# Kernel feature attention and SoLU layer on one core: query maxima joined by a DMA round trip, variance by ScalarE squares

## The chip, the cores and the metric

One core of one Trainium2 chip runs one program. The core has TensorE (PE in the profile, its weight loads PEld), VectorE (DVE), ScalarE (ACT), GpSimd (POOL), SyncE (SP, which here only issues DMAs) and 16 DMA engines. The metric is the device time of one execution in microseconds; lower is better.

## The reference

```python
def phi(x):                                   # x: [8, 8, 576, 64]
    proj = np.einsum('bhsd,df->bhsf', x, w_phi)              # 128 features
    proj = proj - np.max(np.abs(proj), axis=-1, keepdims=True)
    return np.concatenate([np.exp(proj), np.exp(-proj)], axis=-1)
q_p, k_p = phi(q), phi(k)
kv = np.einsum('bhsf,bhsd->bhfd', k_p, v);  z = np.sum(k_p, axis=2)
num = np.einsum('bhsf,bhfd->bhsd', q_p, kv)
den = np.einsum('bhsf,bhf->bhs', q_p, z)[..., None] + 1e-06
x = (num / den)                               # -> 4608 tokens x 512
h = x @ w_in                                  # 512 -> 1024
e = np.exp(h - h.max(-1));  sm = e / (e.sum(-1) + 1e-09);  solu = h * sm
var = np.mean((solu - mu) ** 2, axis=-1)      # mu: mean of solu over 1024
out = ((solu - mu) / np.sqrt(var + 1e-06) * g_ln) @ w_out    # 1024 -> 512
```

## The kernel before

The work has two halves that run interleaved. The attention half goes over 16 units u (a batch and one of two groups of four heads), and each unit has two halves `sub` of two heads each. The second half, called moe in the code, goes over 36 tiles t of 128 tokens. Each step is an `op` with a name, an engine, a cost that a planner had used, and the names of the ops that it follows. The tuple `SEQUENCE` is a list of op numbers: it is the order in which the ops are written into the program, and with it the order of every engine's queue. The same walk gives out the buffers of each tag (`SBUF_BUFS`, `PSUM_BUFS`), so a buffer is reused in that order too. All matrix products in the split parts are made of three `fp32r` products of high and low parts.

Names in the profile: `pjk` is a projection of keys and `pq` one of queries (units 3 to 15, transposed, 128 features on the partitions and 288 tokens along the row). `visit` is one TensorE group per half: `num` and `den` of the half before, `kvT` of this one. `h` is the first product of a moe tile (24 matmuls in two halves), `o` the second one (24 matmuls). `uT` is TensorE's transposition of the last tiles (t from 33); the other tiles are transposed by `ub` (VectorE, 32x32 blocks) and a DMA round trip `du`, `uTs`, and then split into `uhs` and `uls`. The PSUM tag `a` has three banks; `pjk`, `pq`, `num`, `den`, `mtp` and `mcp` share them. The tag `h` has one buffer of two banks, and it is free again when `moe_u` has read it.

The maximum over features for a query half (26 of them, units 3 to 15). VectorE transposes `pq` in 32x32 blocks to `blk`, where a partition p = 32 q + t holds the 32 features of quadrant q of a token t. `q_max4` takes the maximum of absolute values inside each quadrant, `m4` of 128x36. The four quadrants of each token must then meet: `q_mt` transposes `m4` on TensorE (`mtp`), `q_max` takes the maximum over the four (`mt`), `q_mb` copies it four times on GpSimd (`mb`), `q_mc` transposes back on TensorE (`mcp`), and `q_mcol` copies it on ScalarE (`mcol`). `q_sub` subtracts it on GpSimd, VectorE transposes back (`pT`), and ScalarE takes the exponentials `fq` that the next visit reads.

The variance in a moe tile. `moe_u` forms h times e on VectorE (`eu`). `moe_var` takes `bn_stats` of its two halves and `bn_aggr` on VectorE (`bst`, `mv`). `moe_scale` makes, on GpSimd, (variance + (1e-3 (sum + 1e-9))^2) to the power -1/2 in four small instructions (`sa`, `sa`, `sa`, `sc`). Only `moe_oe`, the scaled copy of `o` out of PSUM on ScalarE (`os`), waits for `sc`. The mean itself need not be subtracted there, since `w_out` is centred beforehand.

Of the kernel before, what the change touches and what calls it, by code (L numbers as in the profile page):

```python
# [8 lines left out]
F32 = mybir.dt.float32  # L9
# [11 lines left out]
P = 128  # L21
# [19 lines left out]
    rk=4, rv=5, xh=2, xl=2, m=3, d=3, e=6, za=2, kf=2, q4=5, m4=2, mt=2, mb=2, E=2, dE=2, rb=2,  # L41
    xa=1, xb=1, m2k=5, big=8, nm=2, sm=3, bst=2, mv=2, sa=2, sc=3,
# [242 lines left out]
def linear_attention_then_moe(ctx: ExitStack, tc, qT, qT2, kT, v, w_phi, w_in, g_ln, w_out, out):  # L285
# [54 lines left out]
    nc.gpsimd.memset(ones_half, 0.0)  # L340
    for i in range(2):
        nc.gpsimd.memset(ones_half[i * D : (i + 1) * D, i], 1.0)

    mb_tiles = []
    for i in range(SBUF_BUFS["mb"]):
        mb_tiles.append(const.tile([P, 4, 32], F32, name=f"mb{i}"))
# [921 lines left out]
```

## Time and profile before

| what | value |
|---|---|
| time, median of 3 runs (lowest, highest) | 742.18 us (741.92, 743.12) |
| the profiled execution | 742.26 us, span 740.4 us |
| PE busy | 716.5 us, 97% of the span, 4671 matmuls |
| DVE / ACT / POOL busy | 545.4 / 377.1 / 485.2 us |
| DMA | 109.96 MB, 149 GB/s, 51.7% of 16 engines |

Matmuls overlap in the records: one that is shown with 400 ns starts 0.23 us after its neighbour. The distance between starts, or the chain of waits, tells what a matmul costs the queue; the mean ns of one does not. All lines read L273, since one helper issues every instruction; groups are told apart by the names of tiles.

### The profile page before, as it was taken

Reading aid. Unit: us, or ns where it says so; the run is one execution under the profiler, and the core shown is the slowest. Engines: PE = TensorE matmul, PEld = TensorE weight load, DVE = VectorE, ACT = ScalarE, POOL = GpSimd, SP = SyncE. Lnnn points to the kernel's source line nnn. Section 1 sums busy time; section 2 is a strip of 40 time slices with the busy share of each in tenths; the row PEclk is TensorE's granted clock in tenths of the full one; section 3 lists DMA queues with packets and bytes.
Section 4 is the critical chain, followed back from the end, with each engine's and each line's share of the span. In section 5 each row is a group of like instructions: output and inputs, shape, how many; then the busy total and the mean of one; then the engine's idle time right before and its main releaser. Section 6 shows DMA issues by size and latency. Waiting matters only on the chain. (4 is left out here: it accounts for less than half of the span.)

```text
span 740.4 us, 13275 instructions
## 1 busy us (share of the span) xinstructions
PE 716.5 (97%) x4671; PEld 533.0 (72%) x4671; DVE 545.4 (74%) x861; ACT 377.1 (51%) x717; POOL 485.2 (66%) x507
## 2 busy tenths in 40 slices
PE   6999989999999999999999999999999999999997
PEld 4666767677667777777777777776777677778886
DVE  6999879776768787869769687669777876627651
ACT  3795665544644563645456545535644552424231
POOL 1126799985888878777778885977757867033210
PEclk9999999999999999999999999999999999999999
DMA  7874446652845675555566555563744353511241
GB/s 225 283 239 100 133 131 167 174 156 68 212 112 146 187 212 153 159 136 162 151 172 181 149 153 156 153 191 96 209 130 133 101 161 95 158 40 57 86 150 64
DMA packets 123730, 109.96 MB, mean 149 GB/s; under 512 B 58768, under 2 KB 109968, under 8 KB 123152
## 3 DMA queue, kind: packets, MB, share of 16 engines
q1 hardware_dynamic: 123664, 109.11, 51.7%
q8 instruction: 37, 0.61, 0.4%
q14 instruction: 29, 0.24, 0.1%
HBM read 76.68 MB, written 32.39 MB: 147 GB/s over the span
## 5 line engine op out<-in xcount | busy, mean ns | idle before, releaser
L273 POOL TENSOR_TENSOR zacc<-zacc,ek 128x512 f32<-128x512 f32 (+1 forms) x78 | 107.6, 1379 | 27.4 <-ACT ek L273 23.2
L273 ACT ACTIVATE ek<-dk 128x512 f32<-128x512 f32 (+1 forms) x160 | 90.0, 585 | 51.0 <-DVE dk L273 47.8
L273 PE MATMUL o<-w_out_h,uls 128*128 128x512 f32 x264 | 104.9, 397 | 2.3 <-DVE uls L273 2.3
L273 PE MATMUL o<-w_out_h,uhs 128*128 128x512 f32 x264 | 105.3, 399 | 0.0
L273 PE MATMUL o<-w_out_l,uhs 128*128 128x512 f32 x264 | 104.3, 395 | 0.0
L273 PE MATMUL h<-win_h,mxh 128*128 128x512 f32 x288 | 92.2, 401 | 0.2 <-DVE eu L273 0.2
L273 PE MATMUL h<-win_h,mxl 128*128 128x512 f32 x288 | 90.8, 396 | 0.0
L273 PE MATMUL h<-win_l,mxh 128*128 128x512 f32 x288 | 90.7, 396 | 0.0
L273 ACT ACTIVATE fq<-pT 128x576 f32<-128x576 f32 x104 | 68.5, 679 | 40.2 <-DVE pT L273 39.8
L273 POOL TENSOR_TENSOR hq<-rawq,hq 64x1152 fp32r<-64x1152 f32 x26 | 70.3, 2704 | 6.2 <-ACT hq L273 3.4
L273 ACT ACTIVATE eu<-h,nm 128x1024 f32<-128x1024 f32 x36 | 40.1, 1113 | 66.1 <-DVE nm L273 58.7
L273 DVE TENSOR_TENSOR uls<-uTs,uhs 128x1024 fp32r<-128x1024 f32 x33 | 56.6, 1714 | 20.5 <-ACT uhs L273 19.5
L273 DVE TENSOR_REDUCE m<-pjk 128x4 f32<-128x512 f32 (+1 forms) x80 | 49.4, 620 | 28.2 <-PE pjk L273 27.7
L273 PE MATMUL num<-fq,kvf 128*64 128x288 f32 x512 | 69.2, 412 | 0.4 <-DMA kvf<-dk 0.2
L273 POOL TENSOR_TENSOR xa<-E,rb 128x576 f32<-128x576 f32 (+1 forms) x32 | 30.4, 953 | 58.0 <-DMA rb<-d 36.4
L273 PEld LDWEIGHTS h<-win_h,mxl 128*128 128x128 f32 x288 | 54.4, 189 | 13.1
L273 PE MATMUL kvT<-ek,rawv 128*64 128x256 f32 x512 | 63.8, 380 | 0.0
L273 DVE TENSOR_REDUCE nm<-h 128x1 f32<-128x1024 f32 x36 | 43.6, 1212 | 27.0 <-PE h L273 26.9
L273 PEld LDWEIGHTS h<-win_l,mxh 128*128 128x128 f32 x288 | 54.2, 188 | 13.0
L273 PEld LDWEIGHTS o<-w_out_h,uls 128*128 128x128 f32 x264 | 49.6, 188 | 16.6 <-DVE uls L273 4.9
L273 DVE TENSOR_TENSOR eu<-h,eu 128x1024 f32<-128x1024 f32 x36 | 43.7, 1214 | 23.4 <-ACT eu L273 23.1
L273 POOL TENSOR_TENSOR xl<-rawk,xh 128x256 fp32r<-128x256 f32 (+1 forms) x65 | 46.2, 714 | 21.6 <-ACT xh L273 20.9
(116 smaller groups left out, 1593.4 us busy)
## 6 DMA issues: line engine op xcount, KB each, us to landing
du<-ub SPq DMA_DIRECT2D x33, 512.0 KB, 2.9
uTs<-du SPq DMA_DIRECT2D x132, 128.0 KB, 3.2
rawq<-in_q SPq DMA_DIRECT2D x26, 576.0 KB, 4.7
rb<-d SPq DMA_DIRECT2D x64, 144.0 KB, 3.7
out<-os SPq DMA_DIRECT2D x36, 256.0 KB, 2.7
rawk<-in_k SPq DMA_DIRECT2D x64, 128.0 KB, 2.9
rawv<-in_v SPq DMA_DIRECT2D x64, 128.0 KB, 3.1
dk<-kvs SPq DMA_DIRECT2D x28, 192.0 KB, 2.2
```

Source lines behind the costliest of these rows:

```text
L273: return self.tc.keep_in_program_order(method(*args, **kwargs))
```

## The change

The 26 query maxima meet by a DMA round trip: `q_mout` writes `m4` to a scratch `dm` in DRAM in the order token, quadrant, column; `q_min` reads for each token all four quadrants (144 numbers) into each of the four partitions that need them (`mq4`); `q_max` takes the maximum over the four on VectorE and gives `mcol` at once. Both DMAs are in SP's queue. The two transpositions, the GpSimd copy and the ScalarE copy go. In the moe half `moe_u` becomes a `scalar_tensor_tensor` that also sums its product (`su`); `moe_var` runs on ScalarE: a small product `nb` that makes minus the mean (scaled by 2^-5), and a `Square` of 1024 elements in place over `eu` with its sum `mv`; it follows the transposition that reads `eu`. `moe_denom`, two small instructions on VectorE (`sa`), takes the place of three GpSimd ones; the power stays on GpSimd. Some tags get more buffers (`m4`, `sm`, `bst`, `mv`, `sa`, `sc`, a new `nb`), `mb` goes. `SEQUENCE` is written anew, with 2811 numbers in place of 2827; only its first line is shown, since the numbers tell a reader nothing.

```diff
-    rk=4, rv=5, xh=2, xl=2, m=3, d=3, e=6, za=2, kf=2, q4=5, m4=2, mt=2, mb=2, E=2, dE=2, rb=2,
-    xa=1, xb=1, m2k=5, big=8, nm=2, sm=3, bst=2, mv=2, sa=2, sc=3,
+    rk=4, rv=5, xh=2, xl=2, m=3, d=3, e=6, za=2, kf=2, q4=5, m4=4, mt=2, E=2, dE=2, rb=2,
+    xa=1, xb=1, m2k=5, big=8, nm=2, sm=5, bst=4, nb=3, mv=4, sa=3, sc=4,
...
 SEQUENCE = (
-    3, 95, 0, 2, 136, 102, 132, 7, 97, 105, 140, 98, 133, 99, 88, 89, 106, 103, 107, 137, 117, 134, 135, 8, 144,
+    3, 95, 0, 2, 136, 132, 7, 102, 97, 103, 133, 140, 98, 111, 99, 195, 100, 137, 117, 134, 101, 96, 135, 8,
...
-    def q_mt(st, sub):
-        st["mtp", sub] = bank("a", [P, 512], "mtp")
-        nc.tensor.transpose(out=st["mtp", sub][:NM, :P], in_=st["m4", sub], identity=ident)
+    def q_mout(st, sub):
+        st["dm", sub] = dram.tile([32, 4, NM], F32, tag="dm", name="dm")
+        nc.sync.dma_start(out=st["dm", sub].rearrange("t q c -> q t c"), in_=st["m4", sub])
+
+    def q_min(st, sub):
+        st["mq4", sub] = sb("mt", [P, 4 * NM], name="mq4")
+        src = st["dm", sub].rearrange("t q c -> t (q c)").unsqueeze(0)
+        nc.sync.dma_start(out=st["mq4", sub], in_=src.to_broadcast([4, 32, 4 * NM]))
...
     def q_max(st, sub):
-        st["mt", sub] = sb("mt", [NM, 32])
+        st["mc", sub] = sb("m4", [P, NM], name="mcol")
         nc.vector.tensor_reduce(
-            out=st["mt", sub], in_=st["mtp", sub][:NM, :P].rearrange("c (q t) -> c t q", q=4), axis=AX.X,
-            op=ALU.max,
+            out=st["mc", sub], in_=st["mq4", sub].rearrange("p (q c) -> p c q", q=4), axis=AX.X, op=ALU.max
         )
-    def q_mb(st, sub):
-
-        mb = st["mb", sub] = mb_tiles[plan.slot[st["u"], "mb", sub]]
-        nc.gpsimd.tensor_copy(out=mb[:NM], in_=st["mt", sub].unsqueeze(1).to_broadcast([NM, 4, 32]))
-
-    def q_mc(st, sub):
-        st["mcp", sub] = bank("a", [P, 512], "mcp")
-        nc.tensor.transpose(
-            out=st["mcp", sub][:, :P], in_=st["mb", sub].rearrange("c q t -> c (q t)"), identity=ident
-        )
-
-    def q_mcol(st, sub):
-        st["mc", sub] = sb("m4", [P, NM], name="mcol")
-        nc.scalar.copy(out=st["mc", sub], in_=st["mcp", sub][:, :NM])
...
     def moe_u(t):
-        nc.vector.tensor_tensor(out=M["e", t], in0=M["h", t], in1=M["e", t], op=ALU.mult)
+        M["su", t] = sb("bst", [P, 1], name="su")
+        nc.vector.scalar_tensor_tensor(
+            out=M["e", t], in0=M["h", t], scalar=1.0, in1=M["e", t], op0=ALU.mult, op1=ALU.mult, accum_out=M["su", t]
+        )
     def moe_var(t):
-        st = sb("bst", [P, 2, 6])
-        for i in range(2):
-            nc.vector.bn_stats(out=st[:, i, :], in_=M["e", t][:, i * 512 : (i + 1) * 512])
-        M["mv", t] = sb("mv", [P, 2])
-        nc.vector.bn_aggr(out=M["mv", t], in_=st)
+        nb = sb("nb", [P, 1])
+        M["mv", t] = sb("mv", [P, 1])
+        nc.scalar.mul(out=nb, in_=M["su", t], mul=-(2.0**-15))
+        nc.scalar.activation(
+            out=M["e", t], in_=M["e", t], func=AF.Square, scale=2.0**-5, bias=nb, accum_out=M["mv", t]
+        )
+    def moe_denom(t):
+        a = M["sa", t] = sb("sa", [P, 1])
+        nc.vector.tensor_scalar(out=a, in0=M["sm", t], scalar1=1e-9, scalar2=1e-3, op0=ALU.add, op1=ALU.mult)
+        nc.vector.scalar_tensor_tensor(out=a, in0=a, scalar=a, in1=M["mv", t], op0=ALU.mult, op1=ALU.add)
     def moe_scale(t):
-        a = sb("sa", [P, 1])
         M["sc", t] = sb("sc", [P, 1])
-        nc.gpsimd.tensor_scalar(out=a, in0=M["sm", t], scalar1=1e-9, scalar2=1e-3, op0=ALU.add, op1=ALU.mult)
-        nc.gpsimd.tensor_tensor(out=a, in0=a, in1=a, op=ALU.mult)
-        nc.gpsimd.tensor_tensor(out=a, in0=a, in1=M["mv", t][:, 1:2], op=ALU.add)
-        nc.gpsimd.tensor_tensor(out=M["sc", t], in0=a, in1=neg_half, op=ALU.pow)
+        nc.gpsimd.tensor_tensor(out=M["sc", t], in0=M["sa", t], in1=neg_half, op=ALU.pow)
...
-        op(n("var"), "vector", 2 * dve(512) + 200, z + 12, moe_var, (t,), [n("u")],
-           [("bst", n("bst")), ("mv", n("mv"))], [n("e")])
-        op(n("sc"), "gpsimd", 1340, z + 14, moe_scale, (t,), [n("var")], [("sa", n("sa")), ("sc", n("sc"))],
-           [n("sm"), n("mv")])
+        op(n("var"), "scalar", act(DF) + 168, z + 12, moe_var, (t,),
+           [n("tb")] if t < TURN_PE else [n("t", 0), n("t", 1)], [("nb", n("nb")), ("mv", n("mv"))], [n("e"), n("su")])
+        op(n("sa"), "vector", 310, z + 14, moe_denom, (t,), [n("var")], [("sa", n("sa"))], [n("sm"), n("mv")])
+        op(n("sc"), "gpsimd", 520, z + 14.5, moe_scale, (t,), [n("sa")], [("sc", n("sc"))], [n("sa")])
```

How the change moves instructions is seen at three places. TensorE, before, in unit 14: the last matmul of a key projection, then the transposition of a query half's maxima (`mtp`), a tile's `h`, and two `pq` whose banks come after it.

```order
L273 MATMUL pjk<-wph_h,xl 128x256
L273 MATMUL mtp<-ident,m_6921 36x128
L273 MATMUL h<-win_h,mxh 128x512 x2
L273 MATMUL h<-win_l,mxh 128x512 x2
L273 MATMUL h<-win_h,mxl 128x512 x2
L273 MATMUL h<-win_h,mxh 128x512 x2
L273 MATMUL h<-win_l,mxh 128x512 x2
L273 MATMUL h<-win_h,mxl 128x512 x2
L273 MATMUL pq<-hq,w_hh 128x288
```

TensorE, after, at the like place of unit 14, behind the visit's `den`:

```order
L272 MATMUL den<-fq,kvf 32x288 x8
L272 MATMUL pq<-hq,w_hh 128x288
L272 MATMUL pq<-hq,w_l_88 128x288
L272 MATMUL pjk<-wph_h,xh 128x256
L272 MATMUL pjk<-wph_l,xh 128x256
L272 MATMUL pjk<-wph_h,xl 128x256
```

No transposition stands among the matmuls any more; the groups of `h`, `o`, `pjk`, `pq` and the visits are all there, in much the same rotation.

VectorE, before, from a query half's `q_max4` (`m_6855`) to the maximum over the quadrants (`mt`):

```order
L273 TENSOR_REDUCE m_6855<-blk 128x36
L273 TENSOR_TENSOR uls<-uTs,uhs 128x1024
L273 STREAM_TRANSPOSE blk<-pq 128x288
L273 TENSOR_REDUCE m<-pjk 128x4
L273 TENSOR_REDUCE mt<-mtp 36x32
```

VectorE, after, from `q_max4` of a half (`m_6751`) to its `mcol`, which now waits for a DMA:

```order
L272 TENSOR_REDUCE m_6751<-blk 128x36
L272 STREAM_TRANSPOSE blk<-pq 128x288 x3
L272 TENSOR_REDUCE m_6775<-blk 128x36
L272 TENSOR_REDUCE nm<-h 128x1
L272 TENSOR_TENSOR uls<-uTs,uhs 128x1024
L272 SCALAR_TENSOR_TENSOR eu,su<-h,eu 128x1024
L272 STREAM_TRANSPOSE ub<-eu 128x8x4x32
L272 TENSOR_REDUCE mcol<-mq_6841 128x36
```

More work of VectorE stands between the two maxima than before, and no `bst` or `mv` rows stand among it.

SP's queue, before, around the load of a query half in unit 14 or 15 (`d` and `rb` are the reciprocals of `den`, `vz` and `rawv` values):

```order
L273 DMA rawq<-in_q 128x1152
L273 DMA d_6787<-cmr 128x9
L273 DMA du<-ub 128x1024
L273 DMA rawv<-in_v 128x256
L273 DMA uTs<-du 32x4x256
```

SP's queue, after, with the two round trips of unit 14:

```order
L272 DMA dm<-m_6751 4x32x36
L272 DMA out<-os 128x512
L272 DMA uTs<-du 32x4x256
L272 DMA rb<-d_6621 64x2x288 x2
L272 DMA mq_6841<-dm 128x1x144
L272 DMA dm<-m_6775 4x32x36
L272 DMA uTs<-du 32x4x256
L272 DMA rawq<-in_q 128x1152
L272 DMA mq_6848<-dm 128x1x144
L272 DMA rawv<-in_v 128x256
```

The two DMAs of a round trip stand in the queue with other transfers between them, and whatever comes later waits behind them.

More of the change, by code (lines that the diff above doesn't have):

```diff
@@ L342, in linear_attention_then_moe @@
         nc.gpsimd.memset(ones_half[i * D : (i + 1) * D, i], 1.0)
-    mb_tiles = []
-    for i in range(SBUF_BUFS["mb"]):
-        mb_tiles.append(const.tile([P, 4, 32], F32, name=f"mb{i}"))
-        nc.gpsimd.memset(mb_tiles[i], 0.0)
     win_h = const.tile([P, DM // P, DF], F32R, name="win_h")
@@ L985, in linear_attention_then_moe @@
                 add(("qm4", sub), "vector", dve(2 * S), z, q_max4, (sub,), prev, [("m4", ("m4", sub))], [("blk", sub)])
-                add(("qmt", sub), "tensor", mm(128), z + 0.3, q_mt, (sub,), [("qm4", sub)], [("a", ("mtp", sub))],
-                    [("m4", sub)])
-                add(("qmx", sub), "vector", 200, z + 0.4, q_max, (sub,), [("qmt", sub)], [("mt", ("mt", sub))],
-                    [("mtp", sub)])
-                add(("qmb", sub), "gpsimd", 400, z + 0.5, q_mb, (sub,), [("qmx", sub)], [("mb", ("mb", sub))],
-                    [("mt", sub)])
-                add(("qmc", sub), "tensor", mm(128), z + 0.7, q_mc, (sub,), [("qmb", sub)], [("a", ("mcp", sub))],
-                    [("mb", sub)])
-                add(("qml", sub), "scalar", 90, z + 0.8, q_mcol, (sub,), [("qmc", sub)], [("m4", ("mc", sub))],
-                    [("mcp", sub)])
-                add(("qs", sub), "gpsimd", 2070, z + 1, q_sub, (sub,), [("qml", sub)], (), [("blk", sub), ("mc", sub)])
+                add(("qmo", sub), "sync", (380, 450), z + 0.3, q_mout, (sub,), [("qm4", sub)], (), [("m4", sub)])
+                add(("qmi", sub), "sync", (440, 1000), z + 0.5, q_min, (sub,), [("qmo", sub)], [("mt", ("mt", sub))])
+                add(("qmx", sub), "vector", 230, z + 0.8, q_max, (sub,), [("qmi", sub)], [("m4", ("mc", sub))],
+                    [("mt", sub)])
+                add(("qs", sub), "gpsimd", 2070, z + 1, q_sub, (sub,), [("qmx", sub)], (), [("blk", sub), ("mc", sub)])
             for c in range(2):
@@ L1193, in linear_attention_then_moe @@
            [(e_tag, n("e")), ("sm", n("sm"))], [n("h"), n("nm")])
-        op(n("u"), "vector", dve(DF), z + 7, moe_u, (t,), [n("ex")], (), [n("h"), n("e")])
-        op(n("var"), "vector", 2 * dve(512) + 200, z + 12, moe_var, (t,), [n("u")],
-           [("bst", n("bst")), ("mv", n("mv"))], [n("e")])
-        op(n("sc"), "gpsimd", 1340, z + 14, moe_scale, (t,), [n("var")], [("sa", n("sa")), ("sc", n("sc"))],
-           [n("sm"), n("mv")])
+        op(n("u"), "vector", dve(DF) + 65, z + 7, moe_u, (t,), [n("ex")], [("bst", n("su"))], [n("h"), n("e")])
+        op(n("var"), "scalar", act(DF) + 168, z + 12, moe_var, (t,),
+           [n("tb")] if t < TURN_PE else [n("t", 0), n("t", 1)], [("nb", n("nb")), ("mv", n("mv"))], [n("e"), n("su")])
+        op(n("sa"), "vector", 310, z + 14, moe_denom, (t,), [n("var")], [("sa", n("sa"))], [n("sm"), n("mv")])
+        op(n("sc"), "gpsimd", 520, z + 14.5, moe_scale, (t,), [n("sa")], [("sc", n("sc"))], [n("sa")])
         by_dma = t < TURN_PE
```

293 rows, old and new, of the table SEQUENCE are left out of this document.

## The prediction

> **What bounds the kernel.** I read the page first, for the shares, then the windows, for where TensorE idles, then TensorE's own waits, then the chain of waits, for what one instruction costs the queue, and last the groups.
>
> ```profile
> PE 716.5 (97%) x4671; PEld 533.0 (72%) x4671; DVE 545.4 (74%) x861; ACT 377.1 (51%) x717; POOL 485.2 (66%) x507
> PEclk9999999999999999999999999999999999999999
> ```
>
> TensorE is busy for 97% of the span at the full granted clock; the other engines have a quarter of their time or more free. The windows (PE, PEld, DVE, ACT, POOL busy, granted clock, DMA share, GB/s) say where the rest of TensorE's time is.
>
> ```profile
> 0.00:100.00 100.00, 89.41 (x782) 62.28 (x782) 86.47 (x129) 66.93 (x141) 42.55 (x41) 1.00 0.63 191
> 100.00:640.00 540.00, 531.08 (x3452) 394.84 (x3451) 412.35 (x675) 282.24 (x532) 419.59 (x419) 1.00 0.55 152
> 640.00:700.00 60.00, 59.43 (x281) 46.59 (x281) 30.56 (x35) 17.52 (x30) 18.93 (x34) 1.00 0.27 83
> 700.00:741.00 41.00, 36.62 (x162) 29.32 (x160) 15.97 (x22) 10.40 (x16) 4.10 (x14) 0.98 0.29 97
> ```
>
> TensorE idles 10.6 us in the first 100 us, 8.9 us in the long middle, 0.6 us after it, and about 3.8 us at the very end of the 740.4 us span (the last copy and store). In the middle it is the bound at every moment but 8.9 us. So an instruction taken off TensorE is worth what it occupies there, and work taken off or put on another engine is worth only the waits of TensorE that it ends or makes. The waits by name:
>
> ```profile
> PE pjk L273 <- DMA wph<-in_w_phi: 5.1, 1, 5.1
> PE pq L273 <- DVE mt L273: 2.5, 4, 1.0
> PE dT L273 <- DVE dq L273: 2.3, 2, 1.6
> PE o L273 <- DVE uls L273: 2.3, 3, 1.4
> ...
> PE mcp L273 <- POOL mb L273: 0.6, 1, 0.6
> PE mcp L273 <- DVE dk L273: 0.4, 1, 0.4
> ```
>
> The 5.1 us are the first load and stay. Three rows, 2.5 + 0.6 + 0.4 = 3.5 us, belong to the step that the change replaces: `mcp` waits for GpSimd's copy, and `pq` waits four times until VectorE has read `mt` out of a bank of the three that it shares with `mtp`.
>
> **What a transposition costs TensorE.** The chain of waits, in order of time (start, length, what), has it with and without its neighbours:
>
> ```profile
> 589.85 0.97 PE den L273 x16
> 590.82 0.22 PE mtp L273
> 591.04 0.71 PE pjk L273 x6
> ...
> 609.73 0.97 PE den L273 x16
> 610.70 3.01 PE h L273 x12
> 613.71 0.11 PE mtp L273
> 613.82 0.71 PE pjk L273 x6
> 614.53 2.80 PE h L273 x12
> ...
> 620.14 0.11 PE mcp L273
> ```
>
> Between `fp32r` matmuls one takes 0.11 us. Right behind `den` it shows 0.22 us, but an `h` in that place takes 3.01 us where it takes 2.80 elsewhere: 0.21 us behind `den` are paid by whatever comes next, so there the transposition adds about 0.02. In the order before, 8 of the 52 stand right behind a visit. That makes 44 x 0.11 + 8 x 0.02 = 5.0 us; with 0.11 for all it would be 5.7, the far end.
>
> The groups tell another number for the same instruction:
>
> ```profile
> L273 PE MATMUL mtp<-ident,m 128*36 128x128 f32 x26 | 7.2, 277 | 0.0
> L273 PE MATMUL mcp<-ident,mb 128*128 128x128 f32 x26 | 7.2, 283 | 1.3 <-POOL mb L273 0.6 <-DVE dk L273 0.4
> L273 POOL COPY mb<-mt 36x128 f32<-36x128 f32 x26 | 8.3, 318 | 18.9 <-DVE mt L273 18.8
> L273 DVE TENSOR_REDUCE mt<-mtp 36x32 f32<-36x128 f32 x26 | 6.7, 258 | 2.1 <-PE mtp L273 2.1
> L273 ACT COPY mcol<-mcp 128x36 f32<-128x36 f32 x26 | 4.7, 180 | 17.2 <-PE mcp L273 17.2
> ```
>
> 277 and 283 ns are the time from an instruction's start to its end; the matmuls beside it run meanwhile. I take the spacing in the chain, since it is what delays the next one. [...]
>
> **The other parts, one by one.**
>
> The round trip. The nearest rows are the one of `den`'s reciprocals, a write of small pieces and a read that repeats them over partitions (KB each, median us to landing):
>
> ```profile
> d<-cmr SPq DMA_DIRECT2D x32, 4.5 KB, 2.3
> ...
> rb<-d SPq DMA_DIRECT2D x64, 144.0 KB, 3.7
> ```
>
> 2.3 + 3.7 = 6.0 us, with the issue in it, and a reduction of 144 numbers like `mt` (0.26 us): 6.3 us from `m4` to `mcol`. The path before, from `mtp` at 613.71 to `mcp` at 620.14 in the chain above, took 6.4 us between the two transpositions alone, before `mcol`. So the features `fq` do not come later by it; the likely effect on visits is none or a little slack. A trip under load may take longer; the order shows five or more VectorE instructions between nearly every `m4` and its `mcol`, so a late landing stalls VectorE first, which has 26% free, and TensorE only if that is used up. GpSimd loses 8.3 us of `mb`, ScalarE 4.7 us of `mcol`; neither is the bound, zero each, covered by TensorE's own work.
>
> SP's queue gets 52 DMAs more.
>
> ```profile
> SPq L273 <- DVE ub L273: 99.3, 22, 19.8
> ```
>
> In this one row SP waits 99.3 us for VectorE. Were SP to sit through all of a round trip, 26 x 6.0 = 156 us, it would run out of room; with other transfers between the two DMAs, as the order has them, it sits through a part. What is queued behind a waiting `mq` are loads of keys, values and `uTs`, and behind those `xh`, visits and `uls`. I take zero, and keep the rest as a rival.
>
> The variance and the scale.
>
> ```profile
> L273 DVE BATCH_NORM_STATS2 bst<-eu 128x6 f32<-128x512 f32 x72 | 45.3, 670 | 0.0
> L273 DVE TENSOR_TENSOR eu<-h,eu 128x1024 f32<-128x1024 f32 x36 | 43.7, 1214 | 23.4 <-ACT eu L273 23.1
> L273 ACT ACTIVATE eu<-h,nm 128x1024 f32<-128x1024 f32 x36 | 40.1, 1113 | 66.1 <-DVE nm L273 58.7 <-PE o L273 5.2 <-POOL zacc L273 2.0
> L273 DVE SCALAR_TENSOR_TENSOR w<-wraw,w 128x1024 uint32<-128x1024 uint32 x16 | 19.8, 1236 | 0.0
> L273 POOL TENSOR_TENSOR sa<-sa 128x1 f32<-128x1 f32 x36 | 8.7, 242 | 3.0
> L273 POOL TENSOR_SCALAR sa<-sm 128x1 f32<-128x1 f32 x36 | 7.7, 214 | 2.9
> L273 DVE BATCH_NORM_AGGREGATE mv<-bst 128x2 f32<-128x12 f32 x36 | 7.5, 209 | 2.6 <-DVE bst L273 0.5
> L273 ACT ACTIVATION_READ_ACCUMULATOR eu<-h,nm 128x1 f32 x36 | 6.9, 192 | 0.0
> L273 POOL TENSOR_TENSOR sa<-sa,mv 128x1 f32<-128x1 f32 x36 | 6.8, 190 | 35.6 <-DVE mv L273 33.2
> ...
> L273 ACT ACT_TABLE_LOAD x1 | 1.3, 1283 | 0.7 <-PEq L1258 0.7
> ```
>
> VectorE loses 45.3 + 7.5 = 52.8 us and gains two `sa` instructions of about 0.21 us, like `mv`, 36 times: 15 us. The product op keeps its 1.21 us by the row of `w`, a scalar_tensor_tensor of the same size at 1.24 without a sum; reading the sum may cost from nothing to the 0.19 us of ScalarE's accumulator row, 0 to 7 us in all. VectorE ends near 510 us, 69%. ScalarE gains 36 x (1.11 + 0.19 + 0.18) = 53 us by the rows of the exponential, its accumulator and `mcol` (for `nb`), and ends near 425 us, 57%. GpSimd loses 8.7 + 7.7 + 6.8 = 23.2 us besides `mb`, and ends near 454 us. Nothing here is on TensorE, so each is zero, covered by the 531 us of TensorE work in the middle. The table of ScalarE is loaded once before and, by the order, once after: the squares need no second load.
>
> What comes late next: `bn_stats` waited for nothing (idle 0.0), whereas `sa` now waits in VectorE's queue for ScalarE's squares, and `uh` and `ex` stand behind the squares in ScalarE's queue. The order of everything is new as well. No row shows what waits that makes. From the middle's 8.9 us, 8.9 - 3.5 = 5.4 us are waits outside the replaced step: such an order came to 5.4 us before. A new one could halve them (-2.7) or double them (+5.4). I take +1.0 us, near no change, since the amount of slack between `h`, `o`, the visits and their inputs looks alike in both orders and only the two new queue neighbours speak for more. The first 100 us are reordered too, and are inside the same ends.
>
> **The sum,** against the profiled execution: 742.26 - 5.0 - 3.5 + 1.0 = 734.8 us; it stands 0.08 us above the median of the runs, so 734.7 us for the median.
>
> **Rivals.**
> - The waits come back. `pq` waited for banks; with `mtp` and `mcp` gone the next to hold a bank is another `pq` or `num`, and the new order may wait there. If the 3.5 us return and new waits reach +5.4, the time is 742.2 - 5.0 + 5.4 = 742.6: no change. For it: the order is new everywhere. Against it: 52 bank uses fewer, and VectorE, which empties them, is freer.
> - Slower: SP's queue. If `mq` blocks SP while `dm` is landing, 2.3 us at each of 26 trips, and 0.6 us of that reaches TensorE through late keys or `uTs`, it costs 26 x 0.6 = 15.6 us: 734.7 + 15.6 = 750.3. It decides from 7.5 / 26 = 0.29 us per trip. Against it: the 99.3 us of waiting for `ub` alone, which are room.
> - The transpositions are worth their full 0.28 us: 52 x 0.28 = 14.6 us, so 742.2 - 14.6 - 3.5 + 1.0 = 725.1. Against it: 0.11 in the chain.
> [...]
>
> **How the numbers follow.** The forecast has 0.72: its terms' ends give 742.2 - 5.7 - 3.5 - 2.7 = 730.3 and, with the waits at their worst end, 742.2 - 5.0 - 3.5 + 5.4 = 739.1. Waits that come back have 0.10, SP's queue 0.08, the full price 0.06, the half rate 0.04. From 730.0 to 742.0 lie the forecast, the half rate and half of the first rival: 0.81. A measurement here tells about 0.2%, 1.5 us. Faster than 740.7: 0.70 of the forecast, 0.06 and 0.04, 0.80. Within 0.2%: 0.02 of the forecast and 0.09 of the first rival, 0.11. Slower: 0.01 and 0.08, 0.09.
>
> **What the changed profile would show.** No `mtp`, `mcp` rows; TensorE's busy time near 711 us; no wait of `pq` for `mt`; idle time in the middle near 6 us. DVE near 510, ACT near 425, POOL near 454 us; the product op near 1.2 to 1.3 us; `dm` landing in about 2.3 us and `mq` in 3.7. It would be wrong if TensorE's waits for keys, `uls` or banks grew by more than 5 us, which the list of its waits would show by name.

## The result, and the profile after

The changed kernel is slower: 747.19 us median (13 runs) against 742.12 us for the kernel before in the same runs, a ratio of 1.008 (95% interval 1.0055 to 1.0106). In the profiled execution the time is 745.2 us and the span 743.4 us, where before had 742.26 and 740.4. Ratios here and below are of fast runs alone; of all the runs below only two of `a_poolq`'s six were slow, and they stand in its median.

The page's first rows of the changed kernel, and its clock row:

```profile
PE 712.9 (96%) x4619; PEld 535.6 (72%) x4619; DVE 518.1 (70%) x861; ACT 421.6 (57%) x799; POOL 452.8 (61%) x371
PEclk9999999999999999999999999999999999999999
```

TensorE has 52 instructions fewer and 3.6 us less to do, and the other engines moved about as forecast. So the time did not go into more work of an engine. The windows (PE, PEld, DVE, ACT, POOL busy, granted clock, DMA share, GB/s) show where it went:

```profile
0.00:100.00 100.00, 86.71 (x761) 60.16 (x761) 85.03 (x123) 66.64 (x139) 42.97 (x39) 0.98 0.61 183
100.00:640.00 540.00, 526.73 (x3407) 397.40 (x3407) 393.73 (x677) 315.78 (x592) 393.30 (x313) 1.00 0.57 158
```

TensorE idles 13.3 us in the first 100 us (before 10.6) and 13.3 us in the middle (before 8.9). Its waits by name, in us in total, times, and longest:

```profile
PE num L272 <- DMA kvf<-dk: 6.0, 4, 1.7
PE pjk L272 <- DMA wph<-in_w_phi: 4.8, 1, 4.8
PE pjk L272 <- DMA rawk<-in_k: 2.6, 2, 1.8
PE pq L272 <- POOL hq L272: 1.9, 1, 1.9
PE cmean L272 <- DVE dk L272: 1.9, 1, 1.9
```

The waits of `pq` for `mt` and of `mcp` are gone, as forecast. New at the top is a visit's first product, `num`, waiting for `kvf`: the sums that `kvT` made in an earlier visit, turned by VectorE (`kvs`), written to DRAM (`dk`) and read back in four pieces, all in SP's queue. In the list of before it was one short wait:

```profile
PE num L273 <- DMA kvf<-dk: 0.2, 1, 0.2
```

`rawk` is a load of SP's too. The clock row looks full in 40 slices, but two short windows do not:

```profile
67.10:70.50 3.40, 3.40 (x6) 1.53 (x5) 3.12 (x4) 1.54 (x3) 0.94 (x1) 0.50 0.51 134
101.20:104.60 3.40, 3.40 (x13) 3.21 (x14) 3.33 (x6) 3.37 (x10) 3.32 (x5) 0.51 0.79 218
```

Each stretch of 3.4 us at half clock loses 1.7 us of work, which stands in TensorE's busy time. TensorE's timeline shows what stands ahead of the second one (start, length, what, and the idle time before it):

```profile
97.52 0.49 PE L272 MATMUL dT<-ident,dq 128*128 128x128 f32 x3
99.96 0.40 PE L272 MATMUL pq<-hq,w_hh 128*128 128x288 f32 x1 [1.95 <-POOL hq L272]
...
101.85 0.41 PE L272 MATMUL pjk<-wph_h,xh 128*128 128x256 f32 x1
102.07 0.41 PE L272 MATMUL pjk<-wph_l,xh 128*128 128x256 f32 x1
```

A wait of 1.95 us, and 1.2 us after its end a `pjk` is spaced 0.22 us where it was 0.12 us in the chain before. The groups of the changed operations:

```profile
L272 DVE SCALAR_TENSOR_TENSOR eu<-h,eu 128x1024 f32<-128x1024 f32 x36 | 43.8, 1215 | 22.0 <-ACT eu L272 21.9
L272 ACT ACTIVATE eu<-eu,nb 128x1024 f32<-128x1024 f32 x36 | 41.5, 1152 | 7.3 <-DVE ub L272 4.0 <-PE uT L272 1.5 <-DVE sa L272 0.8
L272 DVE SCALAR_TENSOR_TENSOR sa<-sa,mv 128x1 f32<-128x1 f32 x36 | 20.1, 559 | 14.8 <-ACT eu L272 12.4
L272 DVE TENSOR_REDUCE mcol<-mq 128x36 f32<-128x144 f32 x26 | 10.5, 405 | 13.4 <-DMA mq<-dm 13.4
L272 DVE TENSOR_SCALAR sa<-sm 128x1 f32<-128x1 f32 x36 | 4.6, 129 | 0.0
L272 DVE DVE_READ_ACCUMULATOR eu<-h,eu 128x1 f32 x36 | 3.0, 82 | 0.0
```

And SP's issue of the new DMAs (ns, shortest, median and longest; first and last start):

```profile
L272 SPq DMA_DIRECT2D dm<-m x26: 532/580/802, 106.8 to 612.1; - x26
L272 SPq DMA_DIRECT2D mq<-dm x26: 532/566/593, 109.2 to 617.4; - x26
```

### The profile page after: what moved, and what is told of

It is laid out like the page before. It is cut to its first block, busy times and chain, and to the rows that moved or that the text cites. A ratio compares the mean times of both kernels' runs of the same rounds, so it can differ in the third digit from the quotient of the medians.

```text
span 743.4 us, 13148 instructions
## 1 busy us (share of the span) xinstructions
PE 712.9 (96%) x4619; PEld 535.6 (72%) x4619; DVE 518.1 (70%) x861; ACT 421.6 (57%) x799; POOL 452.8 (61%) x371
## 3 DMA queue, kind: packets, MB, share of 16 engines
q1 hardware_dynamic: 130528, 111.51, 52.6%
## 4 chain that ended last, share of the span: by engine, by line
PE 46%; DMA 7%; DVE 5%; SPq 4%; ACT 2%; issue 2%; POOL 1%; ACTq 0%; DVEq 0%
PE h L272 16%; PE o L272 15%; PE kvT L272 5%; PE num L272 4%; SPq L272 4%; PE pjk L272 3%; DMA uTs<-du 2%; PE den L272 2%; PE pq L272 2%; DMA mq<-dm 1%; DMA kvf<-dk 1%; DMA du<-ub 1%; DVE uls L272 1%; ACT eu L272 1%; POOL zacc L272 1%
## 5 line engine op out<-in xcount | busy, mean ns | idle before, releaser
L272 POOL TENSOR_TENSOR zacc<-zacc,ek 128x512 f32<-128x512 f32 (+1 forms) x78 | 102.0, 1308 | 26.3 <-ACT ek L272 21.7
L272 POOL TENSOR_TENSOR hq<-rawq,hq 64x1152 fp32r<-64x1152 f32 x26 | 71.8, 2761 | 9.2 <-ACT hq L272 3.7
L272 POOL TENSOR_TENSOR blk<-blk,mcol 128x1152 f32<-128x1152 f32 x26 | 56.4, 2167 | 21.8 <-DVE mcol L272 21.7
L272 PEld LDWEIGHTS num<-fq,kvf 128*64 128x64 f32 x512 | 35.3, 137 | 36.7 <-issue 9.8
L272 ACT CAST uhs<-uTs 128x1024 fp32r<-128x1024 f32 x33 | 34.5, 1047 | 47.8 <-DMA uTs<-du 42.7
L272 DVE STREAM_TRANSPOSE blk<-pq 128x288 f32<-128x288 f32 x104 | 46.7, 465 | 20.8 <-PE pq L272 18.3
```

The costliest lines, as they stand in the source:

```text
L272: return self.tc.keep_in_program_order(method(*args, **kwargs))
```

## The experiments

Three theories. A: the loss lies in the re-made order (other places for everything, long early waits and the half clock behind them). B: the 52 DMAs cost, either because SP's queue stands still while `mq` waits for `dm` (B-wait), or because of what they take to issue and move (B-issue), or because `mcol` comes late. C: the squares on ScalarE and `sa` on VectorE delay others in their queues. All the runs in one table (the names `b_` keep the order before, `a_` the changed one; `kvf` is TensorE's wait for it in the profiled execution, halves the stretches at half clock before the end; `b_quad` has no wait for `kvf`):

| run | median us | ratio to before | interval | kvf us | halves |
|---|---|---|---|---|---|
| changed | 747.19 | 1.008 | 1.0055 to 1.0106 | 6.0 | 2 |
| b_q | 744.67 | 1.0039 | 1.0022 to 1.0056 | 4.8 | 0 |
| b_var | 748.35 | 1.0107 | 1.0068 to 1.0146 | 1.8 | 0 |
| b_both | 748.01 | 1.0085 | 1.0055 to 1.0115 | 4.4 | 1 |
| a_nodma | 738.04 | 0.9949 | 0.9925 to 0.9972 | 0.6 | 1 |
| a_unused | 745.76 | 1.0067 | 1.0044 to 1.0089 | 2.9 | 2 |
| a_poolq | 776.2 | 1.04 | 1.034 to 1.0461 | 3.0 | 6 |
| a_novar | 750.57 | 1.0109 | 1.0073 to 1.0145 | 6.3 | 2 |
| a_warm | 756.86 | 1.021 | 1.0174 to 1.0246 | 5.6 | 3 |
| b_late | 746.07 | 1.0077 | 1.0049 to 1.0105 | 6.0 | 1 |
| b_var_nosq | 745.1 | 1.0052 | 1.0025 to 1.0078 | 3.2 | 1 |
| a_nowait | 744.26 | 1.0055 | 1.003 to 1.0081 | 2.1 | 1 |
| a_small | 739.4 | 0.9985 | 0.9965 to 1.0004 | 1.3 | 2 |
| a_actq | 750.91 | 1.0127 | 1.0104 to 1.015 | 3.4 | 1 |
| a_quad | 794.25 | 1.0702 | 1.0676 to 1.0729 | 2.4 | 8 |
| b_quad | 806.88 | 1.088 | 1.0857 to 1.0903 | | 14 |
| b_var_nosa | 749.75 | 1.0114 | 1.0093 to 1.0136 | 3.4 | 2 |
| a_bytes | 742.62 | 0.9989 | 0.996 to 1.0019 | 2.0 | 3 |
| b_nodma | 736.68 | 0.9918 | 0.9891 to 0.9946 | 1.5 | 0 |

Runs of one kernel spread over 2 to 10 us here, so differences are taken between ratios, times 742 us.

**The parts of the change, in the order before.** `b_q` has the round trip alone, `b_var` the variance and scale alone, `b_both` both.

```diff
# b_q: q_mt, q_mb, q_mc, q_mcol go
-        nc.tensor.transpose(out=st["mtp", sub][:NM, :P], in_=st["m4", sub], identity=ident)
+        nc.sync.dma_start(out=st["dm", sub].rearrange("t q c -> q t c"), in_=st["m4", sub])
+        nc.sync.dma_start(out=st["mq4", sub], in_=src.to_broadcast([4, 32, 4 * NM]))
# b_var
-            nc.vector.bn_stats(out=st[:, i, :], in_=M["e", t][:, i * 512 : (i + 1) * 512])
+            out=M["e", t], in_=M["e", t], func=AF.Square, scale=2.0**-5, bias=nb, accum_out=M["mv", t]
```

> The order of before, kept op for op, with the quadrant maxima alone by the DMA round trip: each dm stands in SP's queue where its m4 was ready in the trace of before, each mq about 3.2 us later, each maximum on VectorE about 6.6 us after m4. The variance stays as before. If the loss is in the re-made order (theory A), this gives what the prediction summed for this part: 742.1 - 5.0 - 3.5, so 733 to 738 us, with no half clock after 60 us. If the 52 DMAs in SP's queue make the values kvf late whatever the order (theory B), num waits for kvf by 5 us or more here too and the time is 740 to 746 us. If the variance part is to blame (theory C), this is 733 to 738 us as in A.

> The order of before, kept op for op, with the variance alone by ScalarE squares: each square stands in ScalarE's queue where its transposed tile was ready in the trace of before, sa on VectorE about 2.2 us later, the power on GpSimd behind it. The maxima stay on TensorE. Theory A (re-made order) and theory B (SP's queue): no TensorE work goes or comes, so 740 to 744 us. Theory C (squares in ScalarE's queue and sa in VectorE's queue hold up uh, ex and h's bank): 745 us or more, with new TensorE waits on eu, uls or E.

> The order of before, kept op for op, with both parts of the change put in as in the two runs with one part each. Theory A: 733 to 739 us, faster than both kernels. Theory B: 740 to 746 us, num waits for kvf. Theory C: near 747 us, as the changed kernel.

Each part alone makes the kernel slower though the other operations kept their order, so A alone falls. In `b_q` the wait for `kvf` is at the top again:

```profile
PE num L262 <- DMA kvf<-dk: 4.8, 6, 1.8
SPq L262 <- DMA dm<-m: 22.4, 16, 2.9
```

In the changed kernel SP waits for `dm` far less:

```profile
SPq L272 <- DMA dm<-m: 6.2, 5, 2.0
```

The parts do not add: 0.39% and 1.07% alone, 0.85% together.

**The round trip without its DMAs,** in the changed order. The maximum over the quadrants is left out: `mcol` takes `m4`.

```diff
# a_nodma (q_mout and q_min only return)
-        nc.sync.dma_start(out=st["dm", sub].rearrange("t q c -> q t c"), in_=st["m4", sub])
-        nc.sync.dma_start(out=st["mq4", sub], in_=src.to_broadcast([4, 32, 4 * NM]))
-            out=st["mc", sub], in_=st["mq4", sub].rearrange("p (q c) -> p c q", q=4), axis=AX.X, op=ALU.max
+            out=st["mc", sub], in_=st["m4", sub].unsqueeze(2).to_broadcast([P, NM, 4]), axis=AX.X,
```

> The changed kernel in its own order without the 52 DMAs: the two round trip steps issue nothing, and the maximum on VectorE reads m4 four times over instead (same size, 128x144 to 128x36), so the maximum over quadrants is left out. Theory B: SP's queue is free of them, num no longer waits for kvf, and the time falls by 5 us or more, to 739 to 742 us. Theory A: the early waits with the half clock and the just-in-time visits stay, the time falls by 0 to 3 us, to 744 to 747 us. Theory C: no change, 747 us.

1.008 - 0.9949 = 0.0131: the 52 DMAs carry 9.7 us. The middle then idles 5.9 us, as the windows show:

```profile
100.00:640.00 540.00, 534.08 (x3464) 400.01 (x3463) 393.44 (x683) 318.18 (x594) 395.28 (x316) 1.00 0.56 156
```

**The same without DMAs in the order before,** with the variance of before too; the same maximum is left out. It is `b_q` with the edit of `a_nodma`.

> The order and variance of before, without the two transpositions per query half and without any DMA in their place; mcol takes m4, so the maximum over the quadrants is left out. If the gain predicted for the transpositions is real (5.0 us of TensorE's time and 3.5 us of its waits): 733 to 736. If the waits come back (pq or num waiting for banks): 737 to 739. If the transpositions were free for TensorE: 741 to 743.

```profile
PE 711.4 (97%) x4619; PEld 532.5 (73%) x4619; DVE 543.5 (74%) x861; ACT 374.7 (51%) x691; POOL 481.0 (66%) x479
PE num L262 <- DMA kvf<-dk: 1.5, 4, 0.7
```

TensorE has 716.5 - 711.4 = 5.1 us less to do, and the time falls by 0.0082 x 742 = 6.1 us. From there to `b_q` are 0.0121, 9.0 us for the DMAs, near the 9.7 us of the changed order. The changed order with its variance part costs 0.9949 - 0.9918 = 0.0031, 2.3 us; the interval of this difference reaches zero. In `b_q` TensorE is busy for 713.1 us with the same instructions in the same order and no half clock, so a difference of busy times is good to some 2 us.

**What of the DMAs costs.** `a_unused` issues all 52 but takes `mcol` from `m4`; `a_nowait` reads a piece of the query input in place of `dm`, so nothing waits for a landing; `a_small` cuts both to the 144 bytes of one partition. All three leave the quadrants' maximum out. They also have fewer buffers for `cmp` and `cmr` (3 and 4 for 8), so they are compared with each other first.

```diff
# a_nowait, on top of a_unused
-        src = st["dm", sub].rearrange("t q c -> t (q c)").unsqueeze(0)
+        src = qT[0, 0, :32].rearrange("p j s -> p (j s)")[:, : 4 * NM].unsqueeze(0)
# a_small, on top of a_unused
+        nc.sync.dma_start(out=st["dm", sub][0:1, 0], in_=st["m4", sub][0:1])
+        nc.sync.dma_start(out=st["mq4", sub][0:1, :NM], in_=st["dm", sub][0:1, 0])
```

> The changed kernel with the 52 DMAs issued as they are, but with VectorE's maximum taken from m4 (four times over, as in the kernel without the DMAs), so that nothing waits for what they bring and the maximum over quadrants is left out. Taking the DMAs out altogether gave 738.0 us against 747.2. If what costs is their place in SP's queue (issue times and the wait of mq for dm, with kvf and uTs behind it; theory B1), this stays at 744 to 748 us and num still waits for kvf by 4 us or more. If what costs is that mcol comes late and VectorE's queue and the features behind it with it (theory B2), it falls to 737 to 741 us and the waits for kvf go.

> The changed kernel with all 52 DMAs issued in their places, but the second of each pair reads a piece of the query input, so it waits for no landing; mcol takes m4, so the maximum over the quadrants is left out. Theory B-wait: 738 to 741, SP's wait for dm gone, near the run without the 52 DMAs. Theory B-issue (SP's time to issue, or the packets on the rings): 744 to 747, near the run with the DMAs unused. Theory A: no change to that run either, 744 to 747.

> The changed kernel with all 52 DMAs in their places, the second still waiting for the first, but both cut to the 144 bytes of one partition; mcol takes m4, so the maximum over the quadrants is left out. Theory B-issue (the 128 small pieces of each DMA, in SP's issue time or on the rings): issue well under 0.57 us each, 738 to 741. Theory B-wait (the place in the queue and the wait for the landing): 744 to 747.

`a_unused` keeps 1.0067 of the changed kernel's 1.008, so a late `mcol` is not what mainly costs. Its wait for `kvf` is only 2.9 us, where 4 or more were expected. Not waiting gives back 0.0012, 0.9 us, which is inside the noise. Cutting the pieces gives back 0.0082, 6.1 us, and the wait for `kvf` falls from 2.9 to 1.3 us: by far not all of the 6.1 us. In `a_small` the issue is shorter:

```profile
L272 SPq DMA_DIRECT2D dm<-m x26: 231/246/382, 106.0 to 604.0; - x26
L272 SPq DMA_DIRECT2D mq<-dm x26: 215/284/472, 108.0 to 608.7; - x26
```

**The wait again, in the order before:** `b_late` is `b_q` with `mq` 3 to 7 us later in SP's queue and `mcol` where the order before had it.

> The order before with the q round trip alone (as in the run of that part), but the DMA that reads the maxima back stands some 3 to 7 us later in SP's queue, with more transfers between it and the DMA that writes them, and mcol stands where the order before had it. Theory B-wait (what costs is that SP's queue stands while a round trip lands): SP's wait for dm falls from 22 us to a few, TensorE's wait for kvf under 2 us, time 734 to 740. Theory B-issue (what costs is the time SP takes to issue 52 more DMAs): kvf still waits, 741 to 745. Theory A (the order alone): 736 to 739, as the order is that of before.

```profile
SPq L262 <- DMA dm<-m: 7.4, 6, 2.0
PE num L262 <- DMA kvf<-dk: 6.0, 6, 1.9
```

SP's wait for `dm` fell from 22.4 to 7.4 us, and neither the wait for `kvf` nor the time became better. VectorE now waited 11.1 us for `mq` where it had waited 2.9, so this run alone could hide a gain. But `a_nowait` speaks against B-wait as well, and in the changed kernel SP waits for `dm` for 6.2 us in all, less than the loss. B-wait falls as the main cause.

**Issue time, bytes or pieces.** `a_actq` issues the 52 DMAs from ScalarE's queue, `a_poolq` from GpSimd's. `a_bytes` is `a_small` with the second DMA replaced by a copy of as many bytes as a pair moved, in rows of 4.6 KB, from the query input to DRAM, so the maximum is left out again.

```diff
# a_actq; a_poolq has nc.gpsimd in both
-        nc.sync.dma_start(out=st["dm", sub].rearrange("t q c -> q t c"), in_=st["m4", sub])
+        nc.scalar.dma_start(out=st["dm", sub].rearrange("t q c -> q t c"), in_=st["m4", sub])
# a_bytes
+        nc.sync.dma_start(out=dq, in_=qT[0, 0, :20].rearrange("p j s -> p (j s)"))
```

> The changed kernel with its 52 new DMAs issued from ScalarE's queue, not SP's; same order, same sizes, same packets. Theory B-issue through SP (SP's time to issue): TensorE's wait for kvf falls below 2 us as in the run without the DMAs, and the time to 738 to 742 unless ScalarE's own waits (for dm, about 2 to 3 us at 26 places, before uh, ex or a square) give it back, which TensorE's list would show as waits for E, eu, uhs or mxh. Packets on the rings: kvf still 3 us or more, 744 to 748.

> The changed kernel with the 52 DMAs issued from GpSimd's queue instead of SP's, at the same places in the order. B1: SP is relieved, the waits of num for kvf fall under 2 us, and the time falls to 739 to 744 us, unless GpSimd's own queue, which now waits for m4 and for dm, loses it again. B2: the trip is as long or longer, 747 us or more.

> The changed kernel with the first DMA of each pair cut to one partition's 144 bytes and the second replaced by a copy of 92 KB from the query input to DRAM in 20 rows of 4.6 KB, as many bytes as the pair moved, in few pieces; it waits for no landing, and mcol takes m4, so the maximum over the quadrants is left out. If the small pieces cost through SP's time to issue: issue 0.25 to 0.35 us each and 738 to 741, near the run with small DMAs. If bytes on the rings cost: 743 to 747, near the run that does not wait for the landing.

The DMA queue rows (packets, MB, share of 16 engines) of the changed kernel, of `a_small` and of `a_bytes`, in this order:

```profile
q1 hardware_dynamic: 130528, 111.51, 52.6%
```

```profile
q1 hardware_dynamic: 123768, 109.12, 51.6%
```

```profile
q1 hardware_dynamic: 124548, 111.52, 53.1%
L272 SPq DMA_DIRECT2D dqq<-in_q x26: 509/561/1106, 109.9 to 615.3; - x26
```

`a_bytes` has all the bytes, and its second DMA takes as long to issue as `mq` did, yet its ratio is that of `a_small`, with an interval that does not meet that of `a_nowait`. Its median, 742.62 us, lies between the two expected bands, so some of the cost may be left. Two things differ besides the number of pieces: its copy ends in DRAM, not in SBUF, and its first DMA is issued in 0.26 us instead of 0.58. As for the second, SP spends 29.9 us on issuing the 52 DMAs in `a_unused`, 15.0 in `a_small` and 22.5 in `a_bytes`: half the relief gives the same ratio. That speaks against SP's issue time, but the intervals are too wide to exclude a share of it.

With the issue moved to ScalarE, `kvf` still waits 3.4 us and the kernel is slower than the changed one, but ScalarE itself now waits for these DMAs (7.2 us ahead of `fq` and `mxh`), so that run does not weigh SP's share alone. On GpSimd's queue the time went to 1.04: VectorE waits 37.4 us for `mq`, where it was 13.4, and TensorE 5.8 us for `uls` and 4.2 for `mxl`. That run loses more elsewhere and does not weigh SP's share either.

So the bytes are not the price, as far as a copy to DRAM can tell, and SP's issue time is at most a part of it. What the dear runs of this group with the DMAs from SP share is the number of small pieces, 130,528 - 123,664 = 6,864 packets more than before. By which way these reach TensorE was not isolated. The profiles of the full round trip from SP hold no landing times. Among those with the round trip `a_poolq` alone has them: `dm` 3.1 us, `mq` 3.9 and `kvf` 3.0 in the median, where `kvf` has 2.9 in `a_nodma`.

**The maximum on VectorE.** `a_quad` and `b_quad` take it with four copies and four reductions of 32 partitions, without DMA and with nothing left out.

```diff
+        for q in range(4):
+            nc.vector.tensor_copy(out=st["mq4", sub][:, q], in_=st["m4", sub][32 * q : 32 * q + 32])
+        for q in range(4):
+            nc.vector.tensor_reduce(
+                out=st["mc", sub][32 * q : 32 * q + 32], in_=st["mq4", sub].rearrange("p q c -> p c q"), axis=AX.X,
```

> The changed kernel without the 52 DMAs; the maximum over the four quadrants is taken on VectorE, with four copies of 32 partitions and four reductions to 32 partitions, at mcol's place. Nothing is left out. Theory B (the DMAs cost some 9 us): 737 to 741, TensorE's wait for kvf under 2 us. Rival (VectorE's 26 x 8 short instructions, some 30 to 45 us, delay what TensorE waits for): waits for dk, dq, blk or uls grow, 742 to 746.

> The order and variance of before; only the two transpositions per query half go, and the maximum over the quadrants is taken on VectorE with four copies and four reductions, with no DMA. Nothing is left out. If the predicted gain of the transpositions (5.0 us of TensorE's time and 3.5 us of its waits) is real and the DMAs ate it: 734 to 738. If VectorE, then some 575 to 590 us busy, takes over as what TensorE waits for: 741 to 746.

Both missed the upper end of what was expected, by 48 and 61 us. In `a_quad`:

```profile
L272 DVE TENSOR_REDUCE mcol<-mq 32x36 f32<-32x144 f32 x104 | 41.5, 399 | 2.0
L272 DVE COPY mq<-m 32x36 f32<-32x36 f32 x104 | 41.1, 395 | 1.0
PE pq L272 <- DVE blk L272: 18.0, 6, 5.2
129.60:136.40 6.80, 3.72 (x10) 3.05 (x11) 6.54 (x13) 3.79 (x8) 0.73 (x1) 0.50 0.62 128
```

A reduction of 32 partitions takes 0.40 us, where one of 128 took 0.41 (405 ns), so a block holds VectorE for 8 x 0.40 = 3.2 us, the turns of `blk` stand behind it, and TensorE waits up to 5.2 us at a time. The longest of these waits begins at 127.5 us, and from 129.6 to 136.4 us the granted clock is 0.50 (the last row is a window). TensorE's busy time rose to 731.1 us for the same instructions. These runs do not test B, since they have a bound of their own.

**The variance part.** `a_novar` is the changed kernel without the 36 squares, `b_var_nosq` is `b_var` without them, and `b_var_nosa` has also the `sa` instructions on GpSimd. The variance is left out in all three.

```diff
# a_novar, b_var_nosq
-            out=M["e", t], in_=M["e", t], func=AF.Square, scale=2.0**-5, bias=nb, accum_out=M["mv", t]
+        nc.scalar.mul(out=M["mv", t], in_=M["su", t], mul=2.0**-15)
# b_var_nosa as well
-        nc.vector.scalar_tensor_tensor(out=a, in0=a, scalar=a, in1=M["mv", t], op0=ALU.mult, op1=ALU.add)
+        nc.gpsimd.tensor_tensor(out=a, in0=a, in1=a, op=ALU.mult)
+        nc.gpsimd.tensor_tensor(out=a, in0=a, in1=M["mv", t], op=ALU.add)
```

> The changed kernel without the 36 squares of ScalarE: the small product writes mv, so the variance is left out, and 48 us of ScalarE's work with it (36 x (1152 + 186) ns). Theory C (squares in ScalarE's queue hold up what stands behind them): the time falls by 3 us or more, to 741 to 744 us. Theories A and B: 746 to 748 us.

> The order before with the variance part alone, without the 36 squares: mv is written by the small product on ScalarE instead, so the variance is left out. If ScalarE's 1.15 us square with its accumulator, in a queue with uh and ex, is what cost 7 us there: 743 or less. If it is VectorE's sa, waiting in order for ScalarE, or the places of the new instructions: 746 to 749.

> The order before with the variance part alone, without the squares (the variance is left out, mv is written by the small product) and with the two sa instructions on GpSimd as three, as before. What is left of the part is the product op with its sum, the missing bn_stats and the moved places. If sa in VectorE's queue costs: 742 or less. If the product op's sum or the places cost: 744 to 747, like the run without the squares alone.

Without the squares the changed kernel is no faster, so there the squares are not what costs; `sa` was not taken off VectorE in that order. In the order before the squares may be worth 0.0055, 4 us (the intervals touch), but taking more off VectorE brought the time back up to 749.75 us. No single operation of this part is shown to cost; what makes `b_var` 1.07% slower stays open.

**The half clock.** `a_warm` writes the transpositions ahead of the two early waits six times, to fill them.

```diff
-        for c0, g, t in Q2_PARTS[sub, c]:
+        again = 6 if (st["u"], sub, c, j) in ((1, 1, 0, 1), (2, 1, 0, 0)) else 1
+        for c0, g, t in Q2_PARTS[sub, c] * again:
```

> The changed kernel with two groups of three transpositions, those that stand right before the two long waits of TensorE at 66.7 and 100.0 us, written six times each instead of once, into the same bank with the same values, so that TensorE works through some 1.7 us of each wait. If the half clock that follows each of these waits for 3.4 us is set off by the idle time, both stretches run at the full clock and the time falls by about 3 us, to 743 to 745 us. If it is set off by something else, the half clock stays and the time is 746 to 748 us.

The two early stretches went: the mean granted clock over the first 100 us is 1.00, where the changed kernel has 0.98. Three others came: from 100 to 640 us it is 0.99, where the changed kernel has 1.00. The time rose to 756.86 us. Both expectations missed. That the two stretches went with the idle time fits idle time as what sets them off; why the kernel became 10 us slower is not shown.

## Why the prediction was wrong

- **The transpositions, -5.0: borne out.** `b_nodma`, where they and the copies around them go, has 5.1 us less on TensorE, good to some 2 us. In the changed kernel 3.6 us show, with 2 x 1.7 us of half clock in them; without these it would be 7.0. The rival at their full 0.28 us each, 14.6 us, falls.
- **The waits of the replaced step, -3.5, with new waits at +1.0: the names were right, the sum was not.** The waits for `mt` and `mb` are gone. In `b_nodma` only about 6.1 - 5.1 = 1.0 us of them arrives by the ratio, whose interval allows -1 to 3: waits for `uls` (3.0 us, before 2.3), `ek` (1.5, new) and `kvf` (1.5, before 0.2) come in their place. The +1.0 for new waits lies near the 2.3 us of the rest below, but no row stood behind it; that is luck.
- **"I take zero" for SP's queue: the step that failed.** It measured +9.7 us in the changed order and +9.0 in the order before, 0.37 and 0.35 us per trip where the slower rival decided from 0.29. Its chance, 0.08, leaned on the 99.3 us in which SP waits for `ub`; the runs show that this room did not cover the DMAs. The rival named SP's queue, and late keys or `uTs`; the largest wait that grew is for `kvf` (0.2 to 6.0 us), which the prediction does not name, with `rawk` (2.6 us) behind it. The sign that it gave, waits for keys, `uls` or banks up by more than 5 us, came under another name.
- **That rival's mechanism was wrong too.** SP waiting for `dm` is worth 0.9 us, within the noise (`a_nowait` against `a_unused`), and `b_late` does not speak against it. Cutting the pieces is worth 6.1 us. How they delay TensorE stays open. A `dm` is 18.0 KB and a `mq` 72.0 KB, in 128 pieces each, so a piece has 144 or 576 bytes; no run varies the size of a piece apart from their number.
- **The rest, about 2 us,** is the changed order with its variance part (`a_nodma` against `b_nodma`). The half clock was in no term. In the trace before there is none ahead of the last microseconds (1.00 up to 737 us, 0.83 from there to the end).
- **Engines.** ACT 421.6 against 425, POOL 452.8 against 454, DVE 518.1 against 510. `sa` took 0.56 and 0.13 us, not 0.21 each, and `mcol` 0.41, not 0.26: 36 x 0.27 + 26 x 0.15 = 13.6 us more on VectorE, of which 8.1 show in its total; it has the room. Reading the sum took 0.08 us. The landing of `dm` and `mq`, forecast at 2.3 and 3.7 us, is recorded only in `a_poolq`, from GpSimd's queue, at 3.1 and 3.9.
- **The product op at half rate falls.** No run shows the half rate that has 0.04 in the chances: with the sum, and `h` in PSUM as one source, the op took 1.215 us, against 1.214 before.

With -5.0 and -1.0 from the transpositions, +9.7 from the DMAs and +2.3 from the rest, the sum is +6.0 us; the ratio gives 0.008 x 742 = 5.9. The two agree by construction, since the terms are differences along a chain of runs from before to the changed kernel; what they tell is how the loss is shared out.

## What to carry to other kernels

Waiting time on a queue does not show that more transfers are free there: 52 DMAs of 128 small pieces each cost 9 us on a queue with 99.3 us of waiting in one row, and cutting them to one piece gave back 6. So the pieces of a new transfer are counted, and not only its bytes. The step moved off the bounding engine here saved its occupancy there (5.1 us for 52 transpositions); what takes its place should be run alone, in the old order, before anything is ordered anew. A reduction on 32 partitions was as long as on 128 (0.40 and 0.41 us), so a step cut by quadrants took four reductions for one, and four copies with them.

## What the runs showed of the hardware

- **The granted clock was 0.50 for 3.4 us behind some waits of just under 2 us.** In the changed kernel such stretches start at 67.1 us (0.50) and 101.2 us (0.51), 2.3 and 3.2 us behind the start of TensorE waits of 1.88 and 1.95 us; the wait of 1.78 us that ends at 19.0 us left the clock at 1.00. In `b_q` the longest wait behind the first load is 1.8 us, and the mean clock of the execution is 1.000. `a_nodma` has two waits of 1.9 us and one such stretch: its clock is 0.82 from 64 to 67 us, 0.67 from 67.1 to 70.5 us and 1.00 from 100 to 700 us. From which length of a wait on the clock falls is not shown.
- **A scalar_tensor_tensor on one column,** whose scalar is itself a column, took 0.56 us in the changed kernel, against 0.13 us for the tensor_scalar ahead of it.
- **A copy of 32 x 36 elements between partition quadrants on VectorE** took 0.40 us in `a_quad` and 0.46 in `b_quad`; a reduction of 128 x 144 to 128 x 36 took 0.41 in the changed kernel.
